# Storing a 640-element result as four rows of 320 bytes instead of 128 rows of 10 bytes

## The chip, the cores and the metric

The kernel runs on one core of a Trainium2 chip. The metric is the device time of one execution in microseconds (us); the median of three runs before the change is 684.44 us (684.43 to 684.66). Engines are named as in the profile: PE multiplies matrices (PEld is its weight load), DVE and ACT work element by element, POOL is the general engine, SP issues most of the transfers. SBUF is the on-chip memory of 128 partitions, PSUM the one that PE writes, HBM the memory outside.

## What is computed

One decoding step (one token, width 640) of a transformer block whose normalisations are modulated by a condition vector c: attention of 32 heads over caches of 16,384 keys and values each, then a gated feed-forward of width 1728. All inputs and the output are bf16.

```python
def _A_ref(x, k_cache, v_cache, wq, wo):          # 32 heads, head size 128
    q = (x @ wq) as [heads, 1, 128]
    scores = jnp.einsum('bhqd,bhkd->bhqk', q, k) * Dh ** (-0.5)
    p = _softmax(scores, axis=-1)
    o = jnp.einsum('bhqk,bhkd->bhqd', p, v)
    return o as [1, 32 * 128] @ wo

def _B_ref(x, w_gate, w_up, w_down):
    return (_silu(x @ w_gate) * (x @ w_up)) @ w_down

x = A_x
mod = (_silu(c) @ w_mod).reshape(c.shape[0], 6, 1, -1)
sa, ca, ga, sb, cb, gb = mod[:, 0], ..., mod[:, 5]
h = _layernorm(x) * (1 + ca) + sa
x = x + ga * _A_ref(h, A_k_cache, A_v_cache, A_wq, A_wo)
h = _layernorm(x) * (1 + cb) + sb
x = x + gb * _B_ref(h, B_w_gate, B_w_up, B_w_down)
return x                                           # [1, 1, 640]
```

(Shortened: the reshapes of q and o are written in words.)

## The kernel before

A small planner (`_Plan`) collects operations in program order, each with an engine and a list of operations that it depends on. It gives every engine its operations in that order and turns the dependences into semaphore waits; there is no other scheduling. So the place of an instruction on its engine is the place of its line in `build`.

A vector of 640 is held as 128 partitions of 5: element 5p + k lies in partition p, column k. `KC` is 5.

The stages, in order:

1. Setup. SP issues the loads of `w_mod` and `wq`, ACT those of c and x (one row of 1280 bytes each). POOL makes `ident`, the 128x128 identity (L333). DVE makes constants; among them, in the loop at L391 over the keys of the dictionary `msk` (8, 4, 2), `msk[n]` (L392, 128 x 128/n, has a 1 where p // n equals the column) and `e8[n]` (L397, 128 x n, has a 1 where p % n equals the column). Both are sums over a rearranged `ident`.
2. Modulation and first layer norm. 150 small matmuls (L407) wait for `w_mod`; the next DVE instructions (L412, L415) take their result and make `h_col`, from which the queries are made (L431, L438).
3. Attention, for 16 pairs of heads. The keys of a pair go into one half of `kring` and the values into `vbuf`. DVE multiplies keys by the query and folds the products (L525 to L546), PE sums what is left through `ident` (L516, L554), ACT exponentiates, PE multiplies by the values (L472) into the PSUM bank `acc_ps`. The 14 middle pairs run in a hardware loop on PE.
4. Output projection (L668, L708), residual and second layer norm (L717 to L745).
5. Feed-forward. Gate and up products (L731), the gate (L750 to L756), the down product in four pieces as their weights land (L767), then `tt4` = product times gate (L771) and `o_col` = `tt4` + `x1` (L772), a tile of 128 x 5 in bf16.
6. Store. SP issues the transfer of `o_col` to `out` (L773, through the helper at L80): 128 partitions with 5 elements each, so 128 pieces of 10 bytes. A last operation on SP waits for it (L774), and the program closes.

Other lines that serve the prediction: L640 multiplies a broadcast mask by a broadcast vector on DVE (it makes `Z`), L653 is a matmul of `Z` with `e8[n]`, L560 reduces 256 columns of PSUM on DVE, L564 and L568 are a matmul in f32 and the DVE instruction that takes its result.

Of the kernel before, what the change touches and what calls it, by code (L numbers as in the profile page):

```python
# [6 lines left out]
BF16 = mybir.dt.bfloat16  # L7
F32 = mybir.dt.float32
ALU = mybir.AluOpType
# [28 lines left out]
class _Plan:  # L38
# [28 lines left out]
    def op(self, eng, fn, deps=(), name="", chan=None):  # L67
        o = _Op(eng, fn, list(deps), name, len(self.ops), self.loop.get(eng), chan)
        o.sig = chan is not None
        self.ops.append(o)  # L70
        return o

    def dma(self, out_ap, in_ap, key, deps=(), name="", eng="sp", noncontig=False):
        nc = self.nc

        def fn(e, out_ap=out_ap, in_ap=in_ap, noncontig=noncontig):
            if noncontig:
                with nc.allow_non_contiguous_dma(reason="tiny vector layout change"):
                    return e.dma_start(out_ap, in_ap)
            return e.dma_start(out_ap, in_ap)  # L80

        return self.op(eng, fn, deps, name, chan=self.dma_chan(key))
# [125 lines left out]
def build(nc, A_x, A_k, A_v, A_wq, A_wo, B_wg, B_wu, B_wd, c_in, w_mod, out):  # L208
# [4 lines left out]
    KC = D // 128  # L213
# [15 lines left out]
    with es:  # L229
        block = es.enter_context(nc.Block())  # L230
        plan = _Plan(nc, es)
        op, dma = plan.op, plan.dma
        POOL, ACT, DVE, PE = "pool", "act", "dve", "pe"

        def sb(name, shape, dtype):
            return es.enter_context(nc.sbuf_tensor(name, list(shape), dtype))
# [20 lines left out]
        negid = sb("negid", [128, 64], F32)  # L257
        d2 = sb("d2", [128, 64], F32)
        sel = sb("sel", [128, 8], F32)
        msk = {n: sb("msk%d" % n, [128, 128 // n], F32) for n in (8, 4, 2)}  # L260
        e8 = {n: sb("e%d" % n, [128, n], BF16) for n in (8, 4, 2)}
        Z = sb("Z", [128, H // 8 + 1, 128], BF16)
        A_sb = sb("A_sb", [128, H], BF16)
        rows = qbc[0:1].rearrange("p a d -> p (a d)")[:, 0:2 * D].rearrange("p (j n) -> p j n", j=2)
# [32 lines left out]
        gu_col = sb("gu_col", [128, FCH], BF16)  # L297
        tt4 = sb("tt4", [128, KC], F32)
        o_col = sb("o_col", [128, KC], BF16)

        psb = [es.enter_context(nc.psum_tensor("psb%d" % i, [128, 512], F32)) for i in range(8)]
        S_ps = [psb[0], psb[1]]
        acc_ps = psb[2]
# [30 lines left out]
            out=ident[:], in_=ones_bf[:], pattern=[[1, 128]], compare_op=ALU.is_equal,  # L334
# [27 lines left out]
        def layernorm_ops(src_f32, src_dep, sum_ap, c0, tag, xc_t, free=None, between=None):  # L362
# [26 lines left out]
            out=sel[:], in_=ident[:].rearrange("p (s r) -> p r s", s=4)[:, 0:8, :], axis=AX.X, op=ALU.add), deps=[o_ident], name="sel")  # L389
        o_msk, o_e8 = {}, {}  # L390
        for n in msk:  # L391
            o_msk[n] = op(DVE, lambda e, n=n: e.tensor_reduce(  # L392
                out=msk[n][:], in_=ident[:].rearrange("p (j k) -> p j k", k=n), axis=AX.X, op=ALU.add), deps=[o_ident], name="msk%d" % n)

            def f_e8(e, n=n):
                with nc.allow_low_precision(reason="sum of one 1 and zeros"):
                    return e.tensor_reduce(out=e8[n][:], in_=ident[:].rearrange("p (j k) -> p k j", k=n), axis=AX.X, op=ALU.add)  # L397
            o_e8[n] = op(DVE, f_e8, deps=[o_ident], name="e%d" % n)

        def f_mod(e, m0, m1):
# [10 lines left out]
            out=tt1[:], in0=mod_ps[:, KC:2 * KC], scalar=1.0, in1=xn[:], op0=ALU.add, op1=ALU.mult),  # L413
            deps=[o_mod, o_xn], name="t1")
# [10 lines left out]
        for g in range(H // 4):  # L425
# [10 lines left out]
            for half in range(2):  # L436
                ps = slice(64 * half, 64 * half + 64)
                ev.append(op(ACT, lambda e, g=g, b=b, half=half, ps=ps: e.activation(  # L438
                    out=qbc[ps, 2 * g:2 * g + 2, :],
                    in_=q_ps[b][ps, :].rearrange("p (a h d) -> p a h d", a=2, h=2)[:, :, half, :], func=ACTF.Copy),  # L440
                    deps=[o_q[g]], name="qbc%d_%d" % (g, half)))
# [54 lines left out]
        def diag_last():  # L496

            p, last = NP - 1, o_diag[NP - 2]
            copies = [op(ACT, lambda e, h=h: e.activation(
                out=acc_sb[:, 256 * h:256 * h + 256], in_=acc_ps[:, 256 * h:256 * h + 256], func=ACTF.Copy),  # L500
                deps=[o_pv[p], last], name="acc%d_%d" % (p, h)) for h in range(2)]
            for h in range(2):
                def f_diag(e, h=h):
                    out = None
                    for i in (2 * h, 2 * h + 1):
                        out = e.matmul(OT_ps[:, 0:2], lhsT=acc_sb[:, 128 * i:128 * (i + 1)], rhs=sel[:, i:8:4],  # L506
                                       start=(i == 0), stop=(i == 3))
                    return out
                o_diag[p] = op(PE, f_diag, deps=[copies[h], o_sel, o_ot[p - 1]], name="diag%d_%d" % (p, h))
            return o_diag[p]  # L510
# [90 lines left out]
        while a < len(GROUPS):  # L601
            b = a
            while b < len(GROUPS) and GROUPS[b][1] == GROUPS[a][1]:
                b += 1
            (h0, n), h1 = GROUPS[a], GROUPS[b - 1][0] + GROUPS[b - 1][1]
            d = dma(wo_v[:, h0:h1, :].rearrange("p (g k) n -> p g (k n)", k=n),
                    A_wo[h0 * 128:h1 * 128, :].rearrange("(g p k) n -> p g (k n)", p=128, k=n),
                    ("wo", a), deps=[o_R[NP - 2]], name="dma_wo%d" % a)
            for i in range(a, b):
# [14 lines left out]
                  deps=[o_exp[PL - 1], o_rz, o_onesf, o_rstd], name="La")  # L624
# [4 lines left out]
                  deps=[o_rla] + o_ot[0:NP - 1], name="on")  # L629
# [31 lines left out]
        def project(g):  # L661
            h0, n = GROUPS[g]

            def f_wo(e):
                last = None
                for k in range(h0, h0 + n):
# [11 lines left out]
                  deps=[o_exp[PL], o_rla], name="Lb")  # L678
# [19 lines left out]
        for g in range(NG):  # L698
# [3 lines left out]
                   deps=[o_rl, diag_last()], name="on_last")  # L702

        def f_wol(e):
# [15 lines left out]
            out=x1[:], in0=tt2[:], scalar=1.0, in1=x_f32[:], op0=ALU.mult, op1=ALU.add, accum_out=st[:, 4:5]),  # L720
            deps=[o_ga, o_xf], name="x1")
# [15 lines left out]
        def gate0(o_xc1):  # L737
# [5 lines left out]
            out=tt3[:], in0=xc1[:], scalar=st[:, 7:8], in1=onep_b[:], op0=ALU.mult, op1=ALU.mult),  # L743
            deps=[o_xc1, o_rstd1, o_onep_b], name="t2")
# [25 lines left out]
            prev = op(PE, f_down, deps=[o_gum, d_wd[b], prev, o_nb[NP - 1]], name="down%d" % b)  # L770
        o_t3 = op(DVE, lambda e: e.tensor_tensor(out=tt4[:], in0=f_ps[:, 0:KC], in1=gb, op=ALU.mult), deps=[prev, o_modc], name="gb_ffn")  # L771
        o_oc = op(DVE, lambda e: e.tensor_tensor(out=o_col[:], in0=tt4[:], in1=x1[:], op=ALU.add), deps=[o_t3, o_x1], name="o_col")  # L772
        d_out = dma(out[0, 0].rearrange("(p k) -> p k", p=128), o_col[:], "out", deps=[o_oc], name="dma_out")  # L773
        op("sp", lambda e: e.nop(), deps=[d_out], name="final_wait")  # L774
        plan.emit(block)
    return plan
# [2 lines left out]
def bass_adaLN_cond__gqa_block_cached__swiglu_ffn__decode_kernel(  # L779
    nc: bass.Bass,  # L780
    A_x: bass.AP,
    A_k_cache: bass.AP,
    A_v_cache: bass.AP,
    A_wq: bass.AP,
    A_wo: bass.AP,
    B_x: bass.AP,
    B_w_gate: bass.AP,
    B_w_up: bass.AP,
    B_w_down: bass.AP,
    c: bass.AP,  # L790
    w_mod: bass.AP,
    out: bass.AP,
):
    build(nc, A_x, A_k_cache, A_v_cache, A_wq, A_wo, B_w_gate, B_w_up, B_w_down, c, w_mod, out)
# [28 lines left out]
```

## Time and profile before

| What | us |
|---|---|
| median of three runs | 684.44 |
| the profiled execution, its own time | 684.17 |
| its span, first to last instruction | 682.5 |
| modulation matmuls (L407) begin | 14.97 |
| DVE idle before L412 | 8.55 |
| the last sum, `o_col` (L772), begins | 678.48 |
| store issued | 678.67 |
| store landed (3.4 after its issue) | 682.07 |

The profile is one execution on the chip. A row of the view by line reads: line, engine, operation, output and inputs by name, shape and type, count | busy us in all, mean ns of one | idle us of the engine just before, and what ended that idle time. A row of the timeline reads: start, length, engine, line, operation, and in brackets the idle time before. The chain of waits is followed back from the last instruction to what released each step. A DMA's time "to landing" runs from its issue on the queue to the semaphore update that reports its last byte. Such a transfer is spread over up to sixteen DMA engines, each of which reports by one update of the semaphore.

Busy shares of the span are 55% for PE, 75% for DVE and 7% for ACT; the DMA engines are busy through the whole span but its last slice, with 426 GB/s on average. The granted TensorE clock is 0.595 on average and 0.50 from 670 us on.

### The profile page before, as it was taken

The page shows a single profiled execution, that of the slowest core. Times are in us where ns is not written, and L with a number is a line of the kernel's source. Part 1 is how long each engine was busy: PE and PEld are TensorE (multiplying, and loading weights), DVE is VectorE, ACT ScalarE, POOL GpSimd, SP SyncE. Part 2 cuts the span into 40 slices and gives each one's busy share as a digit, 9 for nine tenths or more (in the row PEclk, how much of TensorE's full clock was granted, in tenths as well). Part 3 has the DMA queues.
Part 4 walks back from the last instruction along what each step waited for, and adds up shares of the span by engine and source line. Part 5 has one row for each costly group of instructions (what it writes and reads, how often), then busy time and mean ns, then how long its engine had stood idle before and what let it go on. Part 6 is the DMA issues. An engine that isn't in the chain of part 4 may idle for free.

```text
span 682.5 us, 5119 instructions
## 1 busy us (share of the span) xinstructions
PE 373.7 (55%) x2282; PEld 154.4 (23%) x2283; DVE 510.8 (75%) x185; ACT 45.5 (7%) x144; POOL 0.7 (0%) x6
## 2 busy tenths in 40 slices
PE   2532275756638183755728174754727275663866
PEld 2311122221212122221212122221302122221535
DVE  2079998959595987959596996959597895999301
ACT  1020000100000000100000000000000000000100
POOL 0000000000000000000000000000000000000000
PEclk9975565655656575655657575555757565565665
DMA  9999999999999999999999999999999999999995
GB/s 384 423 461 427 430 430 431 427 430 431 434 434 434 446 446 438 430 434 430 430 434 430 430 430 434 430 430 430 430 434 434 438 446 442 413 455 392 430 418 222
DMA packets 7711, 290.63 MB, mean 426 GB/s; under 512 B 946, under 2 KB 1204, under 8 KB 2196
## 3 DMA queue, kind: packets, MB, share of 16 engines
q1 hardware_dynamic: 7696, 290.48, 98.8%
q8 instruction: 8, 0.13, 0.1%
q14 instruction: 3, 0.02, 0.0%
q10 hardware_dynamic: 4, 0.00, 0.0%
HBM read 290.47 MB, written 0.00 MB: 426 GB/s over the span
## 4 chain that ended last, share of the span: by engine, by line
DMA 54%; DVE 35%; PE 10%; SPq 0%; issue 0%; ACT 0%
DMA kring<-in_A_k_cache_dram 44%; DVE kring L525 16%; DVE kring L529 8%; PE psb L516 7%; DMA kring<-in_B_w_down_dram 5%; DMA vbuf<-in_A_v_cache_dram 4%; DVE kring L534 4%; DVE kring L540 3%; DVE kring L546 2%; PE psb L472 2%; PE psb L554 1%; SPq L80 0%; DVE pm L560 0%; PE psb L767 0%; PE psb L489 0%
## 5 line engine op out<-in xcount | busy, mean ns | idle before, releaser
L525 DVE TENSOR_TENSOR kring<-kring,qbc 128x16384 bf16<-128x16384 bf16 x28 | 243.2, 8688 | 94.9 <-DMA kring<-in_A_k_cache_dram 94.9
L516 PE MATMUL psb<-kring,ident 128*128 128x256 bf16 x448 | 197.4, 607 | 117.6 <-DVE kring L534 117.6
L529 DVE TENSOR_TENSOR kring<-kring 128x8192 bf16<-128x8192 bf16 x28 | 123.8, 4420 | 0.5
L516 PEld LDWEIGHTS psb<-kring,ident 128*128 128x128 bf16 x448 | 51.5, 120 | 247.6 <-DVE kring L534 127.2
L472 PE MATMUL psb<-vbuf,PZ 128*8 128x512 bf16 x1024 | 91.2, 531 | 11.3 <-DMA vbuf<-in_A_v_cache_dram 11.1
L564 PE MATMUL psb<-d,bd_f 128*128 128x64 f32 x32 | 11.0, 447 | 113.7 <-ACT d L562 113.7
L534 DVE TENSOR_TENSOR kring<-kring 128x4096 bf16<-128x4096 bf16 x28 | 64.0, 2286 | 0.5
L540 DVE TENSOR_TENSOR kring<-kring,qbc 128x16384 bf16<-128x16384 bf16 x4 | 34.7, 8685 | 16.2 <-DMA kring<-in_A_k_cache_dram 16.2
L472 PEld LDWEIGHTS psb<-vbuf,PZ 128*8 128x8 bf16 x1024 | 29.0, 110 | 77.8 <-issue 62.8
L564 PEld LDWEIGHTS psb<-d,bd_f 128*128 128x128 f32 x32 | 8.0, 311 | 115.5 <-DVE pm L560 58.0
L554 PE MATMUL psb<-kring,ident 128*128 128x128 bf16 x64 | 14.5, 393 | 35.0 <-DVE kring L546 35.0
L546 DVE TENSOR_TENSOR kring<-kring 128x8192 bf16<-128x8192 bf16 (+2 forms) x12 | 31.7, 2645 | 0.3
L489 PEld LDWEIGHTS psb<-sel,acc_sb 128*128 128x128 f32 x120 | 27.5, 318 | 7.2 <-issue 4.3
L489 PE MATMUL psb<-sel,acc_sb 128*128 128x2 f32 x120 | 24.5, 326 | 0.7 <-ACT acc_sb L480 0.7
L480 ACT ACTIVATE acc_sb<-psb 128x512 f32<-128x512 f32 x15 | 9.0, 597 | 210.9 <-PE psb L472 210.9
L572 ACT ACTIVATE PZ<-psb,nb 64x256 bf16<-64x256 f32 x32 | 15.0, 468 | 63.0 <-DVE nb L568 62.8
L554 PEld LDWEIGHTS psb<-kring,ident 128*128 128x128 bf16 x64 | 7.5, 122 | 41.4 <-DVE kring L546 36.1
L431 PE MATMUL psb<-vbuf,h_col 128*128 128x512 bf16 x39 | 11.0, 453 | 7.9 <-DMA vbuf<-in_A_wq_dram 7.9
L701 DVE TENSOR_TENSOR A_sb<-psb,rl 128x2 bf16<-128x2 f32 x1 | 0.2, 158 | 19.6 <-PE psb L506 19.6
L562 ACT ACTIVATE d<-negid,pm 128x64 f32<-128x64 f32 x16 | 5.6, 348 | 138.1 <-DVE pm L560 138.0
L493 ACT ACTIVATE OT_sb<-psb 128x2 f32<-128x2 f32 x15 | 2.6, 172 | 152.0 <-PE psb L489 152.0
L407 PE MATMUL psb<-silu_c,kring 128*128 128x1 bf16 x150 | 6.2, 178 | 4.8 <-DMA kring<-in_w_mod_dram 4.8
(93 smaller groups left out, 92.2 us busy)
## 6 DMA issues: line engine op xcount, KB each, us to landing
kring<-in_A_k_cache_dram SPq DMA_DIRECT2D x4, 4096.0 KB, 37.7
vbuf<-in_A_wq_dram SPq DMA_DIRECT2D x1, 5120.0 KB, 27.4
kring<-in_w_mod_dram SPq DMA_DIRECT2D x1, 4800.0 KB, 14.1
vbuf<-in_A_v_cache_dram SPq DMA_DIRECT2D x1, 4096.0 KB, 15.6
kring<-in_A_wo_dram SPq DMA_DIRECT2D x1, 3840.0 KB, 29.2
kring<-in_B_w_gate_dram SPq DMA_DIRECT2D x1, 2160.0 KB, 25.1
vbuf<-in_A_v_cache_dram SPq DMA_DIRECT2D x1, 2048.0 KB, 20.1
kring<-in_B_w_down_dram SPq DMA_DIRECT2D x3, 640.0 KB, 32.5
```

What stands on the lines that cost most here:

```text
L431: last = e.matmul(q_ps[b][:, 0:512], lhsT=h_col[:, k:k + 1].broadcast_to([128, 128]), rhs=wq_v[:, k, g * 512:(g + 1) * 512], start=(k == 0 ...
L472: last = e.matmul(acc_ps[32 * s:32 * s + 8, :], lhsT=PZ[:, p % 2, j, :], rhs=vbuf[:, 4 * j:4 * j + 4, :].rearrange("p t d -> p (t d)"), st ...
L489: last = e.matmul(OT_ps[:, 0:2], lhsT=acc_sb[:, 128 * i:128 * (i + 1)], rhs=sel[:, i:8:4], start=(i == 0), stop=(i == 3))
L516: last = e.matmul(S_ps[p % 2][:, 0:T2], lhsT=ident[:], rhs=kring[:, p % 2, :, d], start=(d == 0), stop=(d == QW + QR - 1))
L525: o_m = op(DVE, lambda e: e.tensor_tensor(out=kv4, in0=kv4, in1=q4, op=ALU.mult), deps=[d_k[p][-1]] + o_qev[p // 2], name="mult%d_%d" % (p ...
L529: o_f = op(DVE, lambda e: e.tensor_tensor(out=kv4[:, :, 0], in0=kv4[:, :, 0], in1=kv4[:, :, 1], op=ALU.add), deps=[o_m], name="fold%d_%d" ...
L534: return op(DVE, lambda e: e.tensor_tensor(out=lo[:, :, 0:QR], in0=lo[:, :, 0:QR], in1=lo[:, :, QR:QW], op=ALU.add), deps=[o_f], name="fol ...
L540: o = op(DVE, lambda e: e.tensor_tensor(out=kv, in0=kv, in1=qbc[:, p, :].unsqueeze(1).broadcast_to([128, KCUT[c + 1] - KCUT[c], 128]), op= ...
L546: o = op(DVE, lambda e, w=w: e.tensor_tensor(out=kv[:, :, 0:w], in0=kv[:, :, 0:w], in1=kv[:, :, w:2 * w], op=ALU.add), deps=[o], name="fol ...
L554: last = e.matmul(S_ps[p % 2][:, KCUT[c]:KCUT[c + 1]], lhsT=ident[:], rhs=kring[:, p % 2, KCUT[c]:KCUT[c + 1], d], start=(d == 0), stop=(d ...
L564: o_mx[p] = op(PE, lambda e: e.matmul(mx_ps[:, 0:64], lhsT=bd_f[:], rhs=d2[:], start=True, stop=True), deps=[o_d2, o_bd1, o_bd2, o_nb[p - ...
L572: o_exp[p] = op(ACT, lambda e, half=half, ps=ps: e.activation(out=PZ[ps, p % 2, :, 4 * half:4 * half + 4], in_=S_ps[p % 2][ps, 0:T2].rearr ...
```

## The change

After `o_col`, the result is rearranged on chip before it is stored. With p = 32q + r, element 5p + k of the result is element 5r + k of row q, so four rows of 160 elements (320 bytes) hold it in order.

- Two more entries of the constants: `msk[32]` (128 x 4: 1 where p // 32 = q) and `e8[32]` (128 x 32: 1 where p % 32 = r), made by the same loop, and `m32`, a bf16 copy of `msk[32]`.
- `o_sp` (128 x 32 x 5): `o_col` repeated 32 times along the middle axis, times `e8[32]` repeated 5 times along the last, so that partition p keeps its five values at r = p % 32 and has zeros elsewhere.
- One matmul with `m32` as weights: row q of the result is the sum over the 32 partitions of group q, which puts each partition's five values at their place. It writes 4 x 160 of `acc_ps`, which is free by then.
- A copy from PSUM into `o_row` (4 x 160, bf16). Each sum has one term that isn't zero, so the values do not change.
- The store takes `o_row`, as four rows.

```diff
-        msk = {n: sb("msk%d" % n, [128, 128 // n], F32) for n in (8, 4, 2)}
-        e8 = {n: sb("e%d" % n, [128, n], BF16) for n in (8, 4, 2)}
+        msk = {n: sb("msk%d" % n, [128, 128 // n], F32) for n in (8, 4, 2, 32)}
+        e8 = {n: sb("e%d" % n, [128, n], BF16) for n in (8, 4, 2, 32)}
...
+        o_sp = sb("o_sp", [128, 32, KC], BF16)
+        o_row = sb("o_row", [4, 32 * KC], BF16)
+        m32 = sb("m32", [128, 4], BF16)
...
+        o_m32 = op(DVE, lambda e: e.tensor_copy(out=m32[:], in_=msk[32][:]), deps=[o_msk[32]], name="m32")
...
-        d_out = dma(out[0, 0].rearrange("(p k) -> p k", p=128), o_col[:], "out", deps=[o_oc], name="dma_out")
+        o_osp = op(DVE, lambda e: e.tensor_tensor(
+            out=o_sp[:], in0=o_col[:].unsqueeze(1).broadcast_to([128, 32, KC]),
+            in1=e8[32][:].unsqueeze(2).broadcast_to([128, 32, KC]), op=ALU.mult), deps=[o_oc, o_e8[32]], name="o_sp")
+        o_om = op(PE, lambda e: e.matmul(acc_ps[0:4, 0:32 * KC], lhsT=m32[:], rhs=o_sp[:].rearrange("p r k -> p (r k)"), start=True, stop=True),
+                  deps=[o_osp, o_m32], name="o_rows")
+        o_or = op(DVE, lambda e: e.tensor_copy(out=o_row[:], in_=acc_ps[0:4, 0:32 * KC]), deps=[o_om], name="o_row")
+        d_out = dma(out[0, 0].rearrange("(q n) -> q n", q=4), o_row[:], "out", deps=[o_or], name="dma_out")
         op("sp", lambda e: e.nop(), deps=[d_out], name="final_wait")
```

## The prediction

> **What bounds the kernel now.** I read the page's chain of waits first, then the end of that chain in order of time, then the tail of the timeline with the waits of SP, and last the rows that price the new instructions. The page's chain (part 4) gives the shares by engine and then by line:
>
> ```profile
> DMA 54%; DVE 35%; PE 10%; SPq 0%; issue 0%; ACT 0%
> DMA kring<-in_A_k_cache_dram 44%; DVE kring L525 16%; DVE kring L529 8%; PE psb L516 7%; DMA kring<-in_B_w_down_dram 5%; DMA vbuf<-in_A_v_cache_dram 4%; DVE kring L534 4%; DVE kring L540 3%; DVE kring L546 2%; PE psb L472 2%; PE psb L554 1%
> ```
>
> The reader is to see that the 682.5 us are a stream of loads with the score arithmetic woven into it. The diff touches none of it: no load, no ring, no order on SP. What it touches stands at the two ends of the program. The chain in order of time ends so (start, length, what):
>
> ```profile
> 643.07 33.49 DMA kring<-in_B_w_down_dram
> 676.56 0.05 issue
> 676.61 0.97 PE psb L767 x20
> 677.58 0.14 issue
> 677.71 0.55 PE psb L767 x10
> 678.26 0.02 issue
> 678.28 0.18 DVE tt L771
> 678.46 0.02 issue
> 678.48 0.17 DVE o_col L772
> ```
>
> Here the last weights have landed and everything is serial: product, gate, residual, store. Nothing else runs, so each microsecond added or removed behind L772 moves the end by as much. The timeline's next line, and the waits of SP in the last 40 us, show the store:
>
> ```profile
> 678.67 0.36 SPq L80 DMA_DIRECT2D out_dram<-o_col  x1
> ```
>
> ```profile
> SPq L80 <- DVE o_col L772: 23.2, 1, 23.2
> SPq L229 <- DMA out_dram<-o_col: 3.0, 1, 3.0
> SPq L229 <- PEq L229: 0.2, 1, 0.2
> ```
>
> SP sets out the store at 678.67 and then waits 3.0 us for it. The answer on the DMA queues puts it at 3.4 us from issue to landing (682.07); closing the program takes to 682.45. Its packets can be seen too: in the view of the queues cut to 679.4 to 680.4 us, 144 packets (128 pieces of 10 bytes and 16 semaphore writes) all move between 679.53 and 679.73. So the 3.4 us are 0.86 from issue to the first packet, 0.20 for all 128 pieces, and 2.34 in which nothing moves and the writes' completion is awaited. The trace's semaphore arrivals part that last stretch further: the sixteen engines report one by one, the first at 680.01 (1.34 after issue), the third and fourth at 680.80, the eighth at 681.46, the last at 682.07.
>
> **The change part by part.** *Removed:* the wait for 128 pieces. *Added on the path:* one masked product on DVE, one matmul, one PSUM copy on DVE, and the wait for four rows of 320 bytes. *Added early:* three small DVE instructions. The prices come from these rows, in the view by line with the shapes kept apart:
>
> ```profile
> L640 DVE TENSOR_TENSOR Z<-msk,on_f 128x128 bf16<-128x128 f32 x5 | 1.1, 287 | 0.0
> L560 DVE TENSOR_REDUCE pm<-psb 128x1 f32<-128x256 f32 x16 | 6.7, 418 | 1.8 <-PE psb L554 1.8
> L717 DVE CAST attn_bf<-psb 128x5 bf16<-128x5 f32 x1 | 0.2, 166 | 0.6 <-PE psb L708 0.6
> L472 PE MATMUL psb<-vbuf,PZ 128*8 128x512 bf16 x1024 | 91.2, 531 | 11.3 <-DMA vbuf<-in_A_v_cache_dram 11.1
> L653 PE MATMUL psb<-e,Z 128*128 128x8 bf16 x3 | 0.2, 174 | 0.0
> L392 DVE TENSOR_REDUCE msk<-ident 128x64 f32<-128x128 bf16 x1 | 0.3, 277 | 0.0
> ```
>
> *The masked product* (128x160, two broadcast operands). L640 is the same operation with one broadcast mask, 128 elements in 287 ns; L772 does 5 in 166. That is 0.98 ns an element, so 160 take 166 + 152 = 0.32 us. Low end 0.25, if it ran at the rate of L529 (4420 ns for 8192, 0.54 ns an element, over L772's floor); high end 0.36 (287 scaled by 160/128). With the 0.03 us that lies between L771 and L772: 0.35.
>
> *The matmul* (weights of 4 columns, 160 columns moved). L653 takes 174 ns at 8 columns and L472 531 at 512, so 0.71 ns a column and 174 + 108 = 0.28 us; a DVE result reaches PE 0.05 later (L756 ends 673.64, L767 starts 673.69). With its weights hidden as in L364, where load and matmul begin together, 0.33; I take 0.35. Low end 0.22 (no cost for columns), high end 0.78 (0.05 and the 0.73 from L564's start to L568's, two passes in f32).
>
> *The copy out of PSUM* (4x160). L717 takes 166 ns for 5 elements, L560 418 for 256, so 1.0 ns an element and 0.32 us; partitions are not what it pays for. With 0.03 from PE to DVE: 0.35. Ends 0.20 and 0.45.
>
> *Together* 0.35 + 0.35 + 0.35 = 1.05 us, from 0.70 to 1.62. The hop from DVE to SP is the one of today (0.02). Each added wait has an empty queue behind it: DVE, PE and SP have no further work, and only the final wait on SP waits for them.
>
> *The early three* (a mask of 4 columns, a mask of 32, a bf16 copy) cost 0.28, up to 0.37 and 0.17 us by L392, L397 and L418, together about 0.7 at the pace they overlap there. They begin where DVE falls idle at 12.6 us; DVE's next instruction, L412, waits until 21.17 for the modulation matmuls on PE, an idle time of 8.55 us. Cost: nothing, with 7.8 us to spare. If the cover were gone they would delay h_col, and so q, by their 0.7 us.
>
> *The store of four rows* is the disputed price: no store of this shape is in the trace. Low end: the load of c, one row of 1280 bytes on one engine, issued at 0.83, has its packet at 1.74 and reports at 2.10: 1.27 us. High end: 3.4, the last of today's engines. Between them it depends on why today's sixteen reports are spread over 2.06 us although all data left within 0.20. Sixteen engines write pieces of 10 bytes that touch each other in memory; if such writes are finished one after another, 128 of them in 2.06 us are 16 ns each, and four would add 0.06 to the first report's 1.34. If an engine's report is late for a reason of its own, four reports are late too. I take 1.7: nearer the first report, since 128 pieces shrink to 4, with 0.3 for larger pieces and the slowest of four. Gain 3.4 - 1.7 = 1.7, from 0 to 2.13.
>
> The page DMA: Bandwidth & Descriptors of the Trainium skill (Anatomy of one DMA) gives a small DMA about 2.0 us whatever its size, most of it the receipt of the write by the target memory. The trace agrees on where the time lies, 2.34 of 3.4 us after the last packet; by that figure the store would gain 1.4 and the kernel 0.35.
>
> *Sum:* 684.17 (the profiled execution's own time, 1.67 above its span of 682.5) + 1.05 - 1.7 = 683.52. The median of the runs, 684.44, lies 0.27 higher; against it, **683.8 us**. All times below are against the median, by landing L and stretch A: 684.44 + A + L - 3.4.
>
> **The rivals.**
> *A. Four rows are as slow as 128 pieces (slower).* Place: the last wait of SP. The report comes late because of the write itself, not because of the number of pieces; then L stays at 3.4, and the stretch is paid in full: 684.44 + 1.05 = 685.49. For it: the pieces take only 0.20 us to move, so their number costs nothing that the packets show. Against it: the first engine with its eight pieces reports at 1.34, so a write can be done early. It decides from L = 2.35 up, where the gain no longer pays 1.05; for a loss of over 0.2% L must exceed 3.72 or A 1.37.
> The same page (Specifications) puts the bound under which a DMA engine reads, modifies and writes at 512 bytes. A row of 320 is below it as a piece of 10 is, so by that rule the reason for slow writes stays, which is rival A; no row of this trace stores a row above or below that size.
> *B. The store has a floor in the middle.* A report on HBM writes never comes as early as the luckiest engine's, but when the third and fourth come today, 2.13. Then 684.44 + 1.05 - 1.27 = 684.22. For it: after 680.80 the reports are evenly dense and only two come before. Against it: all sixteen wrote at the same moment, into the same 1280 bytes.
> *C. All low ends (faster by over 0.2%).* L = 1.27 and A = 0.70 give 684.44 + 0.70 - 2.13 = 683.01. For it: single rows do report so fast in c's load. Against it: that load writes on-chip memory, and DVE rows here all lie near 1 ns an element.
> *D. The change shows up elsewhere,* by moved code or tiles: the big rings are laid out ahead of the new tiles and PE gets one instruction more at its very end, so there is little for it, and no direction.
>
> **How the numbers follow.** The forecast, L from 1.3 to 1.95 and a gain of 0.4 to 1.05 us, has 0.60; B 0.14; A 0.16; C 0.07; D 0.03. Bound for a difference: 0.2% of 684.44 is 1.37 us, more than the forecast can reach with A at 1.05 and L at its low end (-1.08). Faster by over 0.2%: C and a third of D, 0.08. Slower: 0.05 of A (its cases with A over 1.37 or a longer landing) and 0.02 of D, 0.07. Within: 0.60 + 0.14 + 0.11 = 0.85. Range: the forecast spans 683.4 to 684.05; down to 683.1 takes in most of a cheaper stretch, up to 685.2 takes in B and the milder half of A. The forecast's own range with the 0.23 us between the runs shown is 683.2 to 684.3.
>
> **What would show it.** In the profile of the changed kernel: three new DVE rows near 12.5 to 13.3 us, and L415's counterpart still at 21.4 us. Behind the counterpart of L772 a row of about 0.32 us, a matmul of about 0.28, a copy of about 0.32, and the store issued some 1.05 us later than its o_col. In the queues 4 pieces of 320 bytes; from issue to landing 1.7 us, with the first packet again some 0.86 after issue. Wrong is the forecast if landing is above 2.35 (A), the stretch is over 1.3, or the time up to the counterpart of L772 differs by more than the runs do (D).

## The result, and the profile after

| | us |
|---|---|
| before, median of 15 runs | 684.33 (683.82 to 684.71) |
| changed kernel, median of 15 runs beside them | 682.90 (682.72 to 683.04) |
| ratio | 0.9979, 95% interval 0.9972 to 0.9986 |
| profiled execution, before | 684.17, span 682.5 |
| profiled execution, changed | 682.89, span 681.1 |

The kernel became 1.43 us faster, 0.21%. The forecast was 683.8, the lower end of its range 683.1; the measured time lies 0.2 below that end.

The end of the changed kernel's chain of waits in order of time (start, length, what); L776 and L777 are what L771 and L772 were:

```profile
678.09 0.18 DVE tt L776
678.26 0.02 issue
678.29 0.18 DVE o_col L777
678.46 0.02 issue
678.49 0.34 DVE o_sp L778
678.82 0.04 issue
678.87 0.31 PE psb L781
679.17 0.02 issue
679.20 0.31 DVE o_row L783
```

Its timeline has the store, and its waits on SP show how long that was awaited:

```profile
679.54 0.33 SPq L80 DMA_DIRECT2D out_dram<-o_row  x1
```

```profile
SPq L80 <- DVE o_row L783: 24.1, 1, 24.1
SPq L229 <- DMA out_dram<-o_row: 0.8, 1, 0.8
SPq L229 <- PEq L229: 0.2, 1, 0.2
```

The reader is to see two things. Between `o_col` (ends 678.46) and the issue of the store (679.54) there are now 1.08 us where there were 0.02: the stretch costs 1.06. And SP's final wait is 0.8 us where it was 3.0. The trace's semaphore arrivals have the last report at 680.70, 1.16 after issue; before it was 3.40. The spans differ by -1.37 us, which is +1.06, -2.24 for the landing, and -0.19 by which this execution reached `o_col` earlier (678.29 against 678.48).

The added early DVE instructions run in what was idle time, and the instruction behind them starts where it did (21.17 before):

```profile
12.90 0.28 DVE L395 TENSOR_REDUCE msk<-ident 128x4 f32<-128x128 bf16 x1
13.09 0.36 DVE L400 TENSOR_REDUCE e<-ident 128x32 bf16<-128x128 bf16 x1
13.37 0.16 DVE L403 CAST m<-msk 128x4 bf16<-128x4 f32 x1
...
21.18 0.17 DVE L417 SCALAR_TENSOR_TENSOR tt<-psb,xn 128x5 f32<-128x5 f32 x1 [7.66 <-PE psb L412]
```

### The profile page after: what moved, and what is told of

Its sections match the earlier page's. It is cut to its first block, busy times and chain, and to the rows that moved or that the text cites. A ratio compares the mean times of both kernels' runs of the same rounds, so it can differ in the third digit from the quotient of the medians.

```text
span 681.1 us, 5126 instructions
## 1 busy us (share of the span) xinstructions
PE 370.8 (54%) x2283; PEld 154.0 (23%) x2284; DVE 512.0 (75%) x190; ACT 45.5 (7%) x144; POOL 0.7 (0%) x6
## 4 chain that ended last, share of the span: by engine, by line
DMA 54%; DVE 35%; PE 10%; SPq 0%; issue 0%; ACT 0%
DMA kring<-in_A_k_cache_dram 44%; DVE kring L530 17%; DVE kring L534 8%; PE psb L521 7%; DMA kring<-in_B_w_down_dram 5%; DMA vbuf<-in_A_v_cache_dram 4%; DVE kring L539 4%; DVE kring L545 3%; DVE kring L551 2%; PE psb L477 2%; PE psb L559 1%; SPq L80 0%; DVE pm L565 0%; PE psb L772 0%; PE psb L494 0%
## 5 line engine op out<-in xcount | busy, mean ns | idle before, releaser
L477 PE MATMUL psb<-vbuf,PZ 128*8 128x512 bf16 x1024 | 88.5, 519 | 11.9 <-DMA vbuf<-in_A_v_cache_dram 11.8
```

The lines of the kernel that those rows point to most:

```text
L477: last = e.matmul(acc_ps[32 * s:32 * s + 8, :], lhsT=PZ[:, p % 2, j, :], rhs=vbuf[:, 4 * j:4 * j + 4, :].rearrange("p t d -> p (t d)"), st ...
```

## The experiments

So the question is the landing: why four rows report after 1.16 us and 128 pieces after 3.4. Times of the kernel before vary between 683.84 and 684.33 from one group of runs to the next (they ran on different chips), so each run is compared with the kernel before that ran beside it. "Landing" is issue to last report; "after the last packet" is the part of it in which nothing moves any more, from the trace's packets and semaphore arrivals.

**stretch_old_store: the added work, with the old store behind it.**

```diff
-        d_out = dma(out[0, 0].rearrange("(q n) -> q n", q=4), o_row[:], "out", deps=[o_or], name="dma_out")
+        d_out = dma(out[0, 0].rearrange("(p k) -> p k", p=128), o_col[:], "out", deps=[o_or, o_oc], name="dma_out")
```

> The stretch of the change (masked product, matmul, copy) with the store of before behind it: 128 pieces of 10 bytes from o_col, issued when o_row is ready. Theory P (the number of small pieces sets the landing): landing about 3.4 us after issue as before, so the kernel is 1.06 us slower than before, about 685.4. Theory E (the number of engines that report sets it): the same, 685.4. Theory Q (the store of the change lands early because it is issued 1.06 us later, when the loads are further in the past): landing falls here too, to about 2.3 or less, and the kernel stays within 0.3 us of before.

Measured: 685.26 us against 684.28 (ratio 1.0013, 1.0004 to 1.0022). The last line of its timeline and its waits on SP:

```profile
679.84 0.36 SPq L80 DMA_DIRECT2D out_dram<-o_col  x1
```

```profile
SPq L80 <- DVE o_row L783: 24.2, 1, 24.2
SPq L229 <- DMA out_dram<-o_col: 3.3, 1, 3.3
SPq L229 <- PEq L229: 0.2, 1, 0.2
```

The store is issued 1.17 us later than before (1.06 of it is the stretch, the rest lies ahead of it) and awaited for 3.3 us, no shorter than before: Q falls, and the stretch has its price of about 1 us in the whole kernel too. The landing is 3.7 us here and was 3.4 in the first profile, so this store's landing also differs from one execution to another. (The execution profiled here took 685.66 us, the second longest of eleven.)

**pieces128_of_4: the changed kernel with 128 pieces taken from four partitions.**

```diff
-        o_row = sb("o_row", [4, 32 * KC], BF16)
+        o_row = sb("o_row", [4, 32, 8], BF16)
...
+        d_out = dma(out[0, 0].rearrange("(q r k) -> q r k", q=4, k=KC), o_row[:, :, 0:KC], "out", deps=[o_or], name="dma_out")
```

> The changed kernel with o_row laid out with gaps (4 x 32 x 8, five of eight used), so that the store still moves 128 pieces of 10 bytes, but from four partitions. Theory P: landing stays about 3 us or more after issue, the kernel at 685 or more. Theory E, if only four engines report: landing about 1.2 us as in the changed kernel, plus what 32 pieces take on one engine, the kernel at 683.0 to 683.3. Theory Q: 1.2 us, 683.

Measured: 685.28 us against 684.28 (1.0016, 1.0007 to 1.0025). In its timeline the issue on SP alone takes 0.82 us, and its final wait is long again:

```profile
679.49 0.82 SPq L80 DMA_DIRECT2D out_dram<-o_row  x1
```

```profile
SPq L229 <- DMA out_dram<-o_row: 2.7, 1, 2.7
```

Four engines report at the end of it, as in the changed kernel, and the landing is 3.54 us: the first packet 1.42 after issue, 0.61 of moving, and 1.51 after the last packet. With the same number of engines the late report comes back with the pieces (the changed kernel: 0.33 after the last packet). E falls.

**rows16: sixteen rows of 80 bytes.** Every mask for groups of 32 becomes that for groups of 8, so that `o_sp` is 128 x 8 x 5 and `o_row` 16 x 40:

```diff
-        o_sp = sb("o_sp", [128, 32, KC], BF16)
+        o_sp = sb("o_sp", [128, 8, KC], BF16)
...
-        d_out = dma(out[0, 0].rearrange("(q n) -> q n", q=4), o_row[:], "out", deps=[o_or], name="dma_out")
+        d_out = dma(out[0, 0].rearrange("(q n) -> q n", q=16), o_row[:], "out", deps=[o_or], name="dma_out")
```

> The changed kernel with sixteen rows of 80 bytes instead of four of 320 (masks for groups of 8 partitions, which exist already). The stretch gets shorter: masked product 128x40 about 0.20, matmul of 40 columns 0.20, copy 16x40 0.20, hops 0.14, together about 0.75 instead of 1.06. Theory P: sixteen pieces land about as early as four, 1.2 to 1.4 us after issue, and the kernel takes about 682.6, some 0.2 to 0.3 below the changed kernel. Theory E: sixteen engines report as in before, landing 3.0 to 3.4 us, the kernel at 684.4 to 685.

Measured: 682.69 us against 684.28 (0.9976, 0.9967 to 0.9985). The tail of its timeline:

```profile
678.44 0.17 DVE L777 TENSOR_TENSOR o_col<-tt,x 128x5 bf16<-128x5 f32 x1
678.64 0.20 DVE L778 TENSOR_TENSOR o_sp<-o_col,e 128x40 bf16<-128x40 bf16 x1
678.89 0.09 PEld L781 LDWEIGHTS psb<-o_sp,m 128*16 128x16 bf16 x1 [0.77 <-DVE o_sp L778]
678.90 0.20 PE L781 MATMUL psb<-o_sp,m 128*16 128x40 bf16 x1 [0.69 <-DVE o_sp L778]
679.14 0.19 DVE L783 CAST o_row<-psb 16x40 bf16<-16x40 f32 x1 [0.29 <-PE psb L781]
679.35 0.34 SPq L80 DMA_DIRECT2D out_dram<-o_row  x1
```

The stretch from the end of `o_col` (678.61) to the issue is 0.74 us. Sixteen engines report, all of them between 680.51 and 680.67, and the landing is 1.32: sixteen engines are no reason for lateness either.

**rows4_alone: the store of four rows without the stretch.**

```diff
-        o_osp = op(DVE, lambda e: e.tensor_tensor(
...
+        o_or = op(DVE, lambda e: e.tensor_copy(out=o_row[:, 0:KC], in_=o_col[0:4, :]), deps=[o_oc, o_rz0], name="o_row")
```

> The store of four rows without the stretch: o_row is zero but for five columns copied from o_col by one small DVE instruction (0.17 us), so the masked product and the matmul are left out and the output is not the result. Theories P and E: landing 1.16 us after issue as in the changed kernel, so 684.33 + 0.2 - 2.24 = about 682.3, and 0.6 below the changed kernel's 682.9 less what its run-to-run part is. Theory Q: issued 0.85 us earlier than in the changed kernel, the store lands later after its issue, near 2 us, and the kernel is at about 683.

Measured: 681.99 us against 684.28 (0.9967, 0.9955 to 0.9979). The store is issued at 678.67, at the very time of before (`o_col` is reached 0.2 us earlier in this execution, and the small copy takes as much), and lands in 1.17 us. That is nearly the whole gain without its price; the time is 0.3 us below the 682.3 that was expected. Q falls a second time.

So the pieces it is. The next question is what about them: their number, their size, or that they lie against each other. The following kernels store `o_wide` (128 x 32, the result in its first five columns) into a scratch tensor and vary its row pitch, the distance from the start of one row to the start of the next.

**scr_touch, scr_apart, scr_apart64, scr_64.**

```diff
+        o_wide = sb("o_wide", [128, 32], BF16)
+        scratch = nc.dram_tensor("scratch", [128, 5], BF16, kind="Internal").ap()
...
-        d_out = dma(out[0, 0].rearrange("(p k) -> p k", p=128), o_col[:], "out", deps=[o_oc], name="dma_out")
+        d_out = dma(scratch[:, 0:5], o_wide[:, 0:5], "out", deps=[o_oc], name="dma_out")
```

(Shortened: the sum that made `o_col` now writes into `o_wide`, and an early store on ACT's queue sets the output to zeros.) The others differ in the scratch row (256 elements, 32, 32) and, for scr_64, in storing all 32 columns.

> The kernel before, whose last store goes to a scratch tensor in HBM instead of the output (the output is written with zeros at the start, so it is not the result): 128 pieces of 10 bytes that touch each other, as in before. This is the control of the next three. All theories: landing 3.4 to 3.7 us after issue, time within 0.4 us of before.

> As scr_touch, but each piece of 10 bytes stands 512 bytes from the next. Theory T (pieces that touch wait for each other in memory): landing falls to about 1.4 us after issue, since no two pieces share an address range, and the kernel is at about 682.3. Theory S (every small piece has its price, wherever it stands): landing stays at 3 us or more, time within 0.5 us of before.

> As scr_touch, but each piece of 10 bytes stands 64 bytes from the next. Theory T, if the range that pieces wait for is 64 bytes or less: landing about 1.4 us, as in scr_apart; if it is larger, landing between that of scr_apart and 3.4. Theory S: 3 us or more.

> 128 pieces of 64 bytes that follow each other without gaps in scratch (8 KB in all, 27 of 32 elements zeros). If what costs is that a piece covers only a part of its 64 bytes (theory S with a price for partial pieces, or theory T), landing falls to about 1.4 us and the kernel is at about 682.3. If it is the number of pieces as such, landing stays at 3 us or more.

Measured, against 683.93 before: 683.08 (0.9988, 0.9979 to 0.9998), 681.90 (0.9971, 0.9959 to 0.9982), 681.91 (0.9971, 0.9960 to 0.9982) and 681.99 (0.9971, 0.9961 to 0.9981). The answers on the DMA queues, cut to the last 5 us, have one row each for the store (destination and source, queue, count, size, us to landing); the control, then scr_apart, then scr_64:

```profile
scratch<-o_wide SPq DMA_DIRECT2D x1, 1.2 KB, 2.5
```

```profile
scratch<-o_wide SPq DMA_DIRECT2D x1, 1.2 KB, 1.4
```

```profile
scratch<-o_wide SPq DMA_DIRECT2D x1, 8.0 KB, 1.4
```

All four move 128 pieces. Where the pieces stand apart, the same 10 bytes land in 1.4 us; 64 whole bytes need no less. Neither the number of pieces nor their size alone makes the report late. The control missed its expectation: at 2.5 us it lands earlier than the same pieces on the output (3.4 and 3.7), and its time is 0.85 us below that of before, where at most 0.4 was expected. So the touching pieces account for 1.1 us of landing on scratch, less than on the output.

**scr_apart32 and scr_apart16: how far apart is enough.** The scratch row has 16 and 8 elements.

> As scr_apart64, with the pieces of 10 bytes 32 bytes apart, so that two share 64 bytes. If pieces wait for each other within 32 bytes or less: landing 1.4 us as at 64, the kernel at 681.9. If within 64 bytes: two wait for each other instead of six or seven, landing a little later, 1.5 to 1.8, the kernel at 682.0 to 682.3.

> As scr_apart32 with the pieces of 10 bytes 16 bytes apart: two pieces lie in each 32 bytes, where touching pieces put three to four there. If pieces within the same 32 bytes wait for each other: landing between 1.4 and the control's 2.5 us, about 1.6 to 2.0, the kernel at 682.1 to 682.6. If only pieces that touch (or lie closer than 16 bytes) do: 1.4 us as at 32, the kernel at 681.9 to 682.0.

Measured: 682.00 against 683.84 (0.9972, 0.9962 to 0.9983) and 682.01 against 683.84 (0.9974, 0.9963 to 0.9985), landing 1.4 us in both. At these distances two pieces within the same 32 bytes do not make the report late.

**scr_odd42, scr_eight, rows64: touching, or uneven addresses?** At a pitch of 10 bytes the pieces both touch and start anywhere. scr_odd42 has a row of 21 elements, scr_eight a row of 4 (and stores 4 columns), rows64 is the changed kernel with the masks for groups of 2.

> As scr_apart32 with a pitch of 42 bytes: starts are uneven as at a pitch of 10, many pieces cross a multiple of 16 or 32, but 32 bytes lie between one piece and the next. If pieces wait because they touch: landing 1.4 us, the kernel at 682.0. If uneven starts or crossings cost: landing near the control's 2.5 us, the kernel at 683.1.

> 128 pieces of 8 bytes that touch (pitch 8, the fifth column left out of the store): no piece crosses a multiple of 8, but two lie in 16 bytes and four in 32. If pieces wait because they touch or lie within 16 bytes: landing near 2.5 us, the kernel at 683.1. If only uneven starts or crossings cost: 1.4 us, 682.0.

> The changed kernel with 64 rows of 20 bytes (masks for groups of 2): stretch about 0.17 + 0.18 + 0.17 and 0.16 of hops, 0.68 us. The pieces still touch, but there are half as many, and each is twice as long. If the wait goes with the number of pieces that touch: landing between 1.3 and 3.4, near 2.0 to 2.4, the kernel at 683.3 to 683.7 beside 684.2 for before. If rows of 20 bytes do not wait: landing 1.4, 682.7.

Measured, against 683.85 before: 681.96 (0.9972, 0.9961 to 0.9983), 683.43 (0.9994, 0.9984 to 1.0004) and 683.50 (0.9994, 0.9984 to 1.0004). The rows of the queues for scr_odd42, scr_eight and rows64:

```profile
scratch<-o_wide SPq DMA_DIRECT2D x1, 1.2 KB, 1.4
```

```profile
scratch<-o_wide SPq DMA_DIRECT2D x1, 1.0 KB, 3.0
```

```profile
out_dram<-o_row SPq DMA_DIRECT2D x1, 1.2 KB, 2.2
```

The last two times are not clear of noise; what they show is in their traces. Uneven starts cost nothing as long as the pieces stand apart. Pieces of 8 bytes that touch are late, with even starts and though no piece crosses a multiple of 8; at 2.96 they are later than the 2.5 that was expected, but the execution profiled was the slowest of the ten (683.88, median 683.43). Rows of 20 bytes are late on the output too, less so than pieces of 10. The stores side by side:

| Store | pieces x bytes, pitch | landing | after the last packet |
|---|---|---|---|
| output, before | 128 x 10, 10 | 3.40 | 2.33 |
| output, stretch_old_store | 128 x 10, 10 | 3.71 | 2.65 |
| output, pieces128_of_4 | 128 x 10, 10 | 3.54 | 1.51 |
| output, rows64 | 64 x 20, 20 | 2.24 | 0.88 |
| output, rows16 | 16 x 80, 80 | 1.32 | 0.33 |
| output, changed kernel | 4 x 320, 320 | 1.16 | 0.33 |
| scratch, scr_eight | 128 x 8, 8 | 2.96 | 1.92 |
| scratch, scr_touch | 128 x 10, 10 | 2.48 | 1.44 |
| scratch, scr_apart16 | 128 x 10, 16 | 1.41 | 0.37 |
| scratch, scr_odd42 | 128 x 10, 42 | 1.40 | 0.36 |
| scratch, scr_64 | 128 x 64, 64 | 1.41 | 0.36 |

Scr_apart, scr_apart64 and scr_apart32 land in 1.40 to 1.41 us like their neighbours in the table. So stores at pitches of 16, 32, 42, 64, 80, 320 and 512 bytes report 0.33 to 0.37 us after their last packet, touching or not; gap-free pieces of 8, 10 and 20 bytes need 0.9 to 2.7.

One reading fits all rows: pieces that share the same 16 bytes are finished one after another. At the first group of pitches no two pieces share 16 bytes if the tensor starts at a multiple of 16; at 8, 10 and 20 without gaps they do. The reports look like a queue, too: the last five of scr_touch come 1.90, 2.04, 2.19, 2.33 and 2.48 us after issue, in steps of 0.14 to 0.15, where all sixteen of scr_apart come within 0.17 us. But a second reading fits the rows as well: pieces wait when they touch and are shorter than some size between 20 and 64 bytes. Pieces of 16 or 32 bytes without gaps would tell the two apart; they were not tried. Nor were pitches from 11 to 15, where the tensors start was not looked at, and what it is that takes its turn was not found.

**fused16 and after_again: a version that beats both.** From rows16, with the gate and the residual taken out of the tail:

```diff
+        o_gbm = op(DVE, lambda e: e.tensor_tensor(
+            out=gbm[:], in0=gb.unsqueeze(1).broadcast_to([128, 8, KC]),
+            in1=e8[8][:].unsqueeze(2).broadcast_to([128, 8, KC]), op=ALU.mult), deps=[o_modc, o_e8[8]], name="gbm")
...
+            if b == NB - 1:
+                o_xm = op(PE, lambda e: e.matmul(acc_ps[0:16, 0:40], lhsT=m32[:], rhs=x1m[:].rearrange("p r k -> p (r k)"), start=True, stop=False, skip_group_check=True),
...
-        o_t3 = op(DVE, lambda e: e.tensor_tensor(out=tt4[:], in0=f_ps[:, 0:KC], in1=gb, op=ALU.mult), deps=[prev, o_modc], name="gb_ffn")
-        o_oc = op(DVE, lambda e: e.tensor_tensor(out=o_col[:], in0=tt4[:], in1=x1[:], op=ALU.add), deps=[o_t3, o_x1], name="o_col")
...
+            out=o_sp[:], in0=f_ps[:, 0:KC].unsqueeze(1).broadcast_to([128, 8, KC]), in1=gbm[:], op=ALU.mult),
```

> A version meant to beat both: sixteen rows of 80 bytes as in rows16, and the residual is taken out of the tail. The mask is multiplied into the gate gb ahead of time (gbm), the masked x1 is summed into the same PSUM columns by a matmul that runs while PE waits for the third piece of the down weights, and the tail is one product of the PSUM result with gbm, one matmul that adds to it, one copy. Against rows16 this removes two DVE instructions from the tail, 0.20 us each: 682.69 - 0.40 = 682.3, about 2.0 below before. If the early matmul or the two extra DVE products (0.2 us each, while DVE waits for the gate matmuls) delay the chain instead, it is at 682.5 to 682.7.

> The changed kernel itself, beside fused16 on the same chip. Theory: 1.06 us of stretch and a landing 1.16 us after issue, 1.2 to 1.5 below before; fused16 0.5 to 0.65 below this one.

Measured on the same chip, against 683.84 before: fused16 682.12 (682.03 to 682.23; ratio 0.9975, 0.9965 to 0.9984), the changed kernel 682.78 (682.58 to 683.00; 0.9984, 0.9975 to 0.9993). Against the expectations fused16 is 0.66 us below the changed kernel, as thought, but 1.72 below before where about 2.0 was expected, and the changed kernel's own gain is 1.06 here, below the 1.2 to 1.5 that was expected; in the first comparison it was 1.43. The tail of fused16 has three instructions between the last product of the feed-forward and the store:

```profile
677.81 0.20 DVE L788 TENSOR_TENSOR o_sp<-psb,gbm 128x40 bf16<-128x40 f32 x1 [4.51 <-PE psb L784]
678.06 0.09 PEld L791 LDWEIGHTS psb<-o_sp,m 128*16 128x16 bf16 x1 [0.38 <-DVE o_sp L788]
678.06 0.20 PE L791 MATMUL psb<-o_sp,m 128*16 128x40 bf16 x1 [0.29 <-DVE o_sp L788]
678.30 0.19 DVE L793 CAST o_row<-psb 16x40 bf16<-16x40 f32 x1 [0.29 <-PE psb L791]
678.52 0.34 SPq L80 DMA_DIRECT2D out_dram<-o_row  x1
```

From the first of them to the issue 0.71 us; before, L771 and L772 took 0.39 from start to issue. So the rearranged store can be had for 0.3 us instead of 1.06.

## Why the prediction missed

The step that failed is the one called disputed: "I take 1.7", with 1.27 as its low end. The store of four rows landed in 1.16 us, below the low end; the forecast had the direction and the stretch right and this term 0.54 us too long. That is most of the miss, but not all of it. With the measured 1.06 and 1.16 in the prediction's own sum, 684.44 + 1.06 + 1.16 - 3.4, the forecast would have been 683.26, inside the range. Of the 0.36 us from there to the measured 682.90, 0.11 is the median of before, 684.33 in the longer comparison; the other 0.25 stays open. The prediction had given a gain of over 0.2% a chance of 0.08.

- *The stretch.* Forecast 1.05, measured 1.06; the masked product 0.325 (0.32), the matmul 0.294 (0.28), the copy 0.311 (0.32).
- *The early instructions.* Hidden, as worked out: L417 starts at 21.18.
- *The store, direction.* The prediction leaned to the thought that writes which touch each other are finished one after another. The series of pitches shows that gap-free small pieces make the report late, and stretch_old_store, pieces128_of_4 and rows16 show that neither the number of engines nor the moment of issue does. That the pieces wait for each other is the reading of this, not shown itself.
- *The store, size.* The 1.7 is 1.34 for the first report, 0.06 for four writes and 0.3 "for larger pieces and the slowest of four". Measured are 1.10 for the first report, 0.06 from there to the fourth, and nothing for the 0.3. The first report of before, 1.34, was no floor: sixteen rows had theirs at 1.16, and 128 pieces on scratch at 1.24, touching or apart, so more pieces delay it even when they do not crowd. And the low end was taken from c's load, whose issue on ACT took 0.51 us where this one took 0.33; the load's first packet came 0.91 after issue, the store's 0.75. In the profiled executions the sum closes: 684.17 + 1.06 - 2.24 = 682.99, where 682.89 was measured.
- *The store of before.* It was taken as 3.4 from one execution; another execution of the same store took 3.7. A gain read against a landing that varies has that much play: the two comparisons of the changed kernel gave 1.43 and 1.06 us, and the runs of before spread over 0.9 us where those of the changed kernel spread over 0.3. Between the two comparisons the median of before differs by 0.49 us and that of the changed kernel by 0.12, so most of the difference probably lies in what the change takes away; no profile of before from the second group is there to show it.
- *Rival A* fell: the landing shrank to a third. The rule beside it, in DMA: Bandwidth & Descriptors of the Trainium skill (Specifications), that a DMA engine reads, modifies and writes below 512 bytes, does not show as a lateness here (the pieces of before are below that size too): pieces of 10, 64, 80 and 320 bytes all report within 0.37 us of the last packet when they do not crowd each other. No store above 512 bytes was run beside them.
- *Rival B* fell: all sixteen engines of rows16 reported within 1.32 us, so 2.13 was no floor. The figure of about 2.0 us for a small DMA, in the same page of the Trainium skill (Anatomy of one DMA), is too long for this store, and that section is about transfers that the gpsimd engine issues, where SP issues this one; the measured 1.16 decides.
- *Rival C* came near the time (683.01) by luck: the landing was even below its low end, but the stretch was 0.36 us longer than it had. Its counter-argument, that c's load writes on-chip memory, carried no weight: c reports 0.31 us after its packet, the store to HBM 0.33.
- *Rival D* has no support: the product ahead of `o_col` starts at 678.28 us before, and at 678.03 to 678.40 in the four executions profiled with the change up to there (the changed kernel twice, stretch_old_store, pieces128_of_4).

## What to carry to other kernels

A store of a few hundred bytes at the end of a kernel is worth a look at its pieces: if they are of 8 to 20 bytes and follow each other without gaps, their completion is what the program waits for, 0.9 to 2.7 us after the last packet here, though the packets themselves move in 0.2 (0.6 from four partitions). Gathering them on chip pays when it costs less than it saves, and the rows need not be long: rows of 80 bytes did it with a shorter masked product than rows of 320. Work that needs only earlier values, such as a mask times a gate or a residual, can be put into the gather ahead of time.

## What had not been expected

- The completion of an uncrowded write to HBM takes hardly longer than that of a load into on-chip memory: 0.33 us after the last packet against 0.31 for c.
- The same 128 touching pieces land later on the output (2.33 and 2.65 us after the last packet) than on a scratch tensor (1.44). The times beside them agree (683.93 for before, 683.08 for scr_touch on the same chip). Why was not found; on the output, pieces128_of_4 needed 1.51 with its pieces spread over 0.61 us instead of 0.20.
- What an issue costs SP does not follow the number of pieces: 0.82 us for 128 pieces from four partitions, 0.36 for 128 from 128, 0.53 for 64 rows from 64, 0.33 for four rows. It adds to the landing: the first packet comes 1.42, 0.86, 1.18 and 0.75 us after issue. Why 64 rows cost more than 128 pieces was not looked into.
